# Where a discarded output and a normalised tile are kept, in a fused attention and gating kernel

## The chip, the cores and the metric

The kernel runs on one core of a Trainium2 chip. The metric is the device time of one execution in microseconds, read as the median of several executions. The engines have these names in the profile: PE (TensorE, matrix products; PEld is its loading of weights), DVE (VectorE), ACT (ScalarE), POOL (GpSimd) and SP (SyncE, which here only issues DMAs; ACT issues a few as well).

## The reference

Attention with 4 batches of 8 heads, 768 positions and 64 dimensions, in which a query sees only the keys of its own hash bucket, feeds a layer with spatial gating:

```python
q_bucket = sum((q @ proj > 0) * powers);  k_bucket = sum((k @ proj > 0) * powers)
scores = where(q_bucket == k_bucket, q @ k.T / 8, -1e9)
attn = exp(scores - max(scores));  attn = attn / (sum(attn) + 1e-9)
x = (attn @ v), heads side by side                     # 4 x 768 x 512
h = maximum(x @ w_in, 0);  u, v = halves of h          # 512 features each
v_n = (v - mean(v)) / sqrt(var(v) + 1e-6)              # over the features
v_s = w_spatial @ v_n + b_spatial                      # over the positions
out = (u * v_s) @ w_out
```

All inputs and the output are float32.

## The kernel before

**Number format.** Products run in float16, and a float32 operand is carried as two float16 parts, the rounded value and the remainder. Most steps therefore come as a cast on ACT that makes the first part and a subtraction on DVE or POOL that makes the second, called the split here.

**Attention.** There are 32 heads of 6 query tiles each (128 queries by 768 keys). A tile is named by head and row, 13_2 being row 2 of head 13. Heads 1 to 7 (`KEYS`) compute the scores with the keys on the partitions (`scores_k`) and need no transpose. Head 0 and heads 8 to 31, 150 tiles, go through `scores` and `weighted`:

1. L291 and L292: four products on PE put the scores into a PSUM tile `sp` (two of them).
2. L293: DVE scales `sp` by a negative constant and takes the minimum of each row into `nb`. The instruction also has to write its elementwise output somewhere: that is `jk`, a bfloat16 tile that nobody reads. There is one of it.
3. L295: ACT takes the exponential of `sp` with the bias `nb` into `ex`, float32, three buffers (`EB`).
4. L298 and L299: the cast on ACT and the split, on DVE or POOL, write the two halves of `pp`, three buffers (`PB`). POOL has rows 0 and 3 of heads below 16, and row 2 from head 16 on.
5. L301: SP issues a DMA that transposes `pp` into `pt`, five buffers (`PTB`). Heads 1 to 7 keep their exponentials under the same tag.
6. L314 to L316: 18 products on PE multiply `pt` with the values. They stand five tiles (`LAG`) behind the scores in the program.

**Gating layer.** When the 8 heads of a batch are done, `mlp_units` gives 28 units, which are dealt out among the tiles of the next batch. The last batch's units come after all attention. Six units (L361 to L370) make the half v: products, a rectifier on ACT (L365) into `v32m` (four buffers, which the output tiles of L436 use as well), then the statistics on DVE. After three of them `norm` normalises: DVE writes the result into `vy`, two buffers (L388), ACT casts it to the first part of `vn` (L389) and POOL subtracts to the second (L390). The other units make u (L402), the spatial product (L417) and the output (L432).

**Order.** The program is written tile by tile, and each step has a priority that the function `at` sets. A scheduler then fixes the order of the instructions on each engine when the program is built. A tile of a pool that has `bufs` buffers waits for the last reader of the tile `bufs` allocations earlier. On the chip each engine works through its own list in order and waits by semaphores.

Of the kernel before, what the change touches and what calls it, by code (L numbers as in the profile page):

```python
# [10 lines left out]
BF16 = mybir.dt.bfloat16  # L11
F32 = mybir.dt.float32
# [3 lines left out]
ALU = mybir.AluOpType  # L16
# [3 lines left out]
P = 128  # L20
# [16 lines left out]
def lsh_attention_spatial_gating(  # L37
# [11 lines left out]
    nc = tc.nc  # L49
    B, NPAIR, _, _, S = kq.shape  # L50
    NH = 2 * NPAIR
    NT = S // P
    HS = S // 2
    DM = NPAIR * P
    DF = w_in.shape[1]
    F2 = DF // 2
    NF = F2 // P
    ISQ = 1.0 / (SQ * SQ * 8.0)

    VYB = 2  # L60
    QKB = 1
    PSB = (2,2,2)
    MT = "m"
# [2 lines left out]
    wk = ctx.enter_context(tc.tile_pool(name="wk", bufs=1))  # L66
# [189 lines left out]
    def scores_k(n, i):  # L256
# [3 lines left out]
        for c in range(2):  # L260
            cs = slice(c * HS, (c + 1) * HS)
            nc.tensor.matmul(ps[:, c], lhsT=t[:, 1, ks], rhs=t[:, 0, cs], start=True, stop=False)  # L262
            nc.tensor.matmul(ps[:, c], lhsT=t[:, 2, ks], rhs=t[:, 3, cs], start=False, stop=True)  # L263
        ex = wk.tile([P, S], F32, tag="pt", bufs=PTB, name=f"ex{n}_{i}")
        st["ex", n, i] = nc.scalar.activation(ex.rearrange("p (c q) -> p c q", c=2), ps, AF.Exp, scale=ISQ).ins
# [12 lines left out]
    def scores(n, i):  # L278
        if n in KEYS:
            scores_k(n, i)  # L280
            return
        t = ab[n % NAB]
        if i == 0:
            st["nb", n] = wk.tile([P, NT], F32, tag="nb", bufs=3, name=f"nb{n}")
        nb = st["nb", n][:, i:i + 1]
        jk = wk.tile([P, 2, HS], BF16, tag="jk", name=f"jk{n}_{i}")
        qs = slice(i * P, (i + 1) * P)
        ps = ps_sc.tile([P, 2, 512], F32, tag="sc", name=f"sp{n}_{i}")[:, :, :HS]
        for c in range(2):
            cs = slice(c * HS, (c + 1) * HS)  # L290
            nc.tensor.matmul(ps[:, c], lhsT=t[:, 0, qs], rhs=t[:, 1, cs], start=True, stop=False)  # L291
            nc.tensor.matmul(ps[:, c], lhsT=t[0:P - 1, 3, qs], rhs=t[0:P - 1, 2, cs], start=False, stop=True)  # L292
        nc.vector.tensor_scalar(jk, ps, -ISQ, None, op0=ALU.mult, op1=ALU.min, accum_out=nb)  # L293
        ex = wk.tile([P, 2, HS], F32, tag="ex", bufs=EB, name=f"ex{n}_{i}")
        st["ex", n, i] = nc.scalar.activation(ex, ps, AF.Exp, bias=nb, scale=ISQ).ins  # L295
        at(NT * n + i + G_H, 50)
        pp = wk.tile([P, 2, 2, HS], F16, tag="pp", bufs=PB, name=f"pp{n}_{i}")
        nc.scalar.copy(pp[:, 0], ex)  # L298
        (nc.gpsimd if i in (PL_POOL if n >= 2 * NH else PL_POOL1) else nc.vector).tensor_tensor(out=pp[:, 1], in0=ex, in1=pp[:, 0], op=ALU.subtract)  # L299
        pt = st["pt", n, i] = wk.tile([P, 2 * NT, P], F16, tag="pt", bufs=PTB, name=f"pt{n}_{i}")  # L300
        st["tr"] = nc.sync.dma_start_transpose(out=pt, in_=pp.rearrange("p g c k -> p (g c k)")).ins  # L301
# [48 lines left out]
    def mlp_units(b):  # L350
        xt = [st["xt", b * NPAIR + r] for r in range(NPAIR)]
        vn = [wk.tile([P, NT, F2], F16, tag=f"vn{g}", name=f"vn{b}_{g}") for g in range(2)]
        mv = {}
        v32 = {}

        def v_unit(i):
            ps = ps_m.tile([P, 512], F32, tag=MT, name=f"vps{b}_{i}")
            k = 0
            for c in range(NPAIR):
                for gx, gw in THREE:  # L360
                    nc.tensor.matmul(ps, lhsT=xt[c][:, gx, i * P:(i + 1) * P], rhs=wi[gw][:, c, F2:DF],  # L361
                                     start=(k == 0), stop=(k == 3 * NPAIR - 1))
                    k += 1
            v32[i] = wk.tile([P, F2], F32, tag="v32m", bufs=4, name=f"vr{b}_{i}")
            nc.scalar.activation(v32[i], ps, AF.Relu, scale=1.0 / (SX * SX))  # L365
            if i % 3 == 0:
                mv[i // 3] = wk.tile([P, 3, 2], F32, tag="mv", bufs=2, name=f"mv{b}_{i}")
            bs = wk.tile([P, 6], F32, tag="bs", bufs=2, name=f"bs{b}_{i}")
            nc.vector.bn_stats(bs, v32[i])
            nc.vector.bn_aggr(mv[i // 3][:, i % 3, :], bs)  # L370
            if i % 3 == 2:
                norm(i // 3)

        def norm(g):
            m = mv[g]
            ve = wk.tile([P, 3], F32, tag="ve", bufs=2, name=f"ve{b}_{g}")
            nc.vector.tensor_scalar(ve, m[:, :, 1], EPS_LN, None, op0=ALU.add)
            r = wk.tile([P, 3], F32, tag="rs", bufs=2, name=f"rs{b}_{g}")
            nc.scalar.activation(r, ve, AF.Ln)
            nc.scalar.activation(r, r, AF.Exp, scale=-0.5)  # L380

            nc.vector.tensor_mul(ve, ve, r)
            nc.vector.scalar_tensor_tensor(out=ve, in0=ve, scalar=-0.5 * SN, in1=r, op0=ALU.mult, op1=ALU.mult)
            nc.vector.scalar_tensor_tensor(out=r, in0=ve, scalar=1.5 * SN, in1=r, op0=ALU.add, op1=ALU.mult)
            for j in range(3):
                i = 3 * g + j
                y = wk.tile([P, F2], F32, tag="vy", bufs=VYB, name=f"vy{b}_{i}")
                nc.vector.tensor_scalar(y, v32[i], m[:, j, 0:1], r[:, j:j + 1], op0=ALU.subtract, op1=ALU.mult)  # L388
                nc.scalar.copy(vn[0][:, i], y)  # L389
                nc.gpsimd.tensor_tensor(out=vn[1][:, i], in0=y, in1=vn[0][:, i], op=ALU.subtract)  # L390

        u = {}

        def u_unit(d, h):
            if h not in u:
                u[h] = wk.tile([P, NF, HS], F32, tag="u", name=f"u{b}_{h}")
            hs = slice(h * HS, (h + 1) * HS)
            ps = ps_m.tile([P, 512], F32, tag=MT, name=f"ups{b}_{d}_{h}")
            k = 0
            for c in range(NPAIR):  # L400
                for gw, gx in THREE:
                    nc.tensor.matmul(ps[:, :HS], lhsT=wi[gw][:, c, d * P:(d + 1) * P], rhs=xt[c][:, gx, hs],  # L402
                                     start=(k == 0), stop=(k == 3 * NPAIR - 1))
                    k += 1
            nc.scalar.activation(u[h][:, d], ps[:, :HS], AF.Relu, scale=1.0 / SX)  # L405

        gt = {}

        def s_unit(d, h):
            if h not in gt:  # L410
                gt[h] = [wk.tile([P, NF, HS], F16, tag=f"g{g}", name=f"g{b}_{g}_{h}") for g in range(2)]
            hs = slice(h * HS, (h + 1) * HS)
            ps = ps_m.tile([P, 512], F32, tag=MT, name=f"sps{b}_{d}_{h}")
            k = 0
            for c in range(NT):
                for gv, gw in THREE:
                    nc.tensor.matmul(ps[:, :HS], lhsT=vn[gv][:, c, d * P:(d + 1) * P], rhs=ws[gw][:, c, hs],  # L417
                                     start=(k == 0), stop=(k == 3 * NT - 1))
                    k += 1
            y = wk.tile([P, HS], F32, tag="sy", bufs=2, name=f"sy{b}_{d}_{h}")  # L420
            nc.vector.scalar_tensor_tensor(out=y, in0=ps[:, :HS], scalar=1.0 / (SN * SW), in1=bt[:, hs], op0=ALU.mult, op1=ALU.add)  # L421
            nc.gpsimd.tensor_mul(y, y, u[h][:, d])  # L422
            nc.scalar.copy(gt[h][0][:, d], y)
            nc.gpsimd.tensor_tensor(out=gt[h][1][:, d], in0=y, in1=gt[h][0][:, d], op=ALU.subtract)

        def o_unit(i):
            h, j = divmod(i, NT // 2)
            ps = ps_m.tile([P, 512], F32, tag=MT, name=f"ops{b}_{i}")
            k = 0
            for c in range(NF):  # L430
                for gg, gw in THREE:
                    nc.tensor.matmul(ps, lhsT=gt[h][gg][:, c, j * P:(j + 1) * P], rhs=wo[gw][:, c, :],  # L432
                                     start=(k == 0), stop=(k == 3 * NF - 1))
                    k += 1
            o = wk.tile([P, DM], F32, tag="v32m", bufs=4, name=f"o{b}_{i}")
            nc.scalar.activation(o, ps, AF.Copy, scale=1.0 / (SX * SX))  # L436
            nc.sync.dma_start(out=out[b, i * P:(i + 1) * P, :], in_=o)

        units = [lambda i=i: v_unit(i) for i in range(NT)]
        for h in range(2):  # L440
            units += [lambda d=d, h=h: u_unit(d, h) for d in range(NF)]
            units += [lambda d=d, h=h: s_unit(d, h) for d in range(NF)]
            units += [lambda i=i: o_unit(i) for i in range(h * NT // 2, (h + 1) * NT // 2)]
        return units
# [17 lines left out]
        return 99  # L462

    RB = 3
    PB = 3
    EB = 3
    PTB = 5
    XTB = 6
    LAG = 5
    XL_ENG = nc.vector  # L470
# [33 lines left out]
    for g in range(N * NT + LAG):  # L504
        n, i = divmod(g, NT)
        if n < N:
            at(g + G_S, 0)
            scores(n, i)
            r = n // 2
# [38 lines left out]
        while wv < N * NT and wv + (LAGK if wv // NT in KEYS else LAG) <= g:  # L548
            m, j = divmod(wv, NT)
# [64 lines left out]
```

## Time and profile before

| | |
|---|---|
| three executions | 738.57 us median (736.13 to 741.49) |
| span of the profiled execution | 741.7 us |
| PE busy | 631.5 us (85%) |
| DVE busy | 520.6 us (70%) |
| ACT busy | 434.8 us (59%) |
| POOL busy | 321.2 us (43%) |
| DMA moved | 120.95 MB, 163 GB/s in the mean |
| L293, minimum into `jk` | 150 on DVE, 949 ns each |
| L295, exponential | 150 on ACT, 897 ns each |
| L298, cast into `pp` | 150 on ACT, 829 ns each |
| L299, split into `pp` | 116 on DVE, 1089 ns each; 34 on POOL, 1708 ns each |
| L388, normalised v into `vy` | 24 on DVE, 860 ns each |
| L390, second part of `vn` | 24 on POOL, 1300 ns each |

Busy time is the time in which at least one instruction of the engine ran. The profiled execution is one of its own. Its span lies 3.1 us above the median of the three executions. Where a row of the profile says how long an engine idled, the name behind the arrow is the event that came last before the engine went on.

### The profile page before, as it was taken

The numbers are of one execution on the slowest core, as the hardware profiler recorded it, in microseconds if no ns is written. First come the engines' busy times: TensorE is split into PE (matmuls) and PEld (weight loads), VectorE is DVE, ScalarE is ACT, GpSimd is POOL, SyncE is SP. The second block draws the span as 40 slices with busy tenths as digits, with TensorE's granted clock in tenths as the row PEclk, the third lists the DMA queues.
The fourth block names the chain that finished last, engine by engine and source line by source line (L and its number), as shares of the span: only waits on it lengthen the run. The fifth ranks groups of instructions, "written<-read, shape, count | busy, mean of one in ns | idle before, by whom it ended". The sixth has DMA issues, their size and how long they took to land.

```text
span 741.7 us, 14927 instructions
## 1 busy us (share of the span) xinstructions
PE 631.5 (85%) x5759; PEld 400.4 (54%) x5759; DVE 520.6 (70%) x945; ACT 434.8 (59%) x668; POOL 321.2 (43%) x324
## 2 busy tenths in 40 slices
PE   1569898998988776997898899889898998999997
PEld 0237686776445444554544555556455565654553
DVE  4677795536799999567689798678698987755200
ACT  1344574346788676655676577667677776743221
POOL 5122443123458675264314565156235571451503
PEclk9768797999999989898999999999999999999999
DMA  9565554324999989996999799999999999860011
GB/s 235 149 123 155 133 148 102 99 55 97 224 237 197 215 207 187 213 178 138 234 202 199 138 210 213 211 211 212 206 210 181 194 175 213 182 136 15 1 42 43
DMA packets 290011, 120.95 MB, mean 163 GB/s; under 512 B 270740, under 2 KB 273812, under 8 KB 289940
## 3 DMA queue, kind: packets, MB, share of 16 engines
q1 hardware_dynamic: 287636, 119.11, 76.4%
q10 hardware_dynamic: 2304, 0.89, 0.5%
q8 instruction: 45, 0.74, 0.4%
q14 instruction: 26, 0.21, 0.1%
HBM read 28.33 MB, written 6.29 MB: 47 GB/s over the span
## 4 chain that ended last, share of the span: by engine, by line
PE 43%; DMA 21%; DVE 13%; issue 8%; ACT 6%; POOL 6%; SPq 3%; ACTq 0%; DVEq 0%; POOLq 0%
DMA pt<-pp 14%; PE pv L275 6%; PE vps L361 6%; PE ops L432 5%; PE sps L417 5%; PE ups L402 5%; DMA ab<-hl 4%; PE sp L291 3%; DVE jk L293 3%; PE sp L292 3%; DVE pp L299 2%; PE sp L262 2%; PE pv L314 2%; ACT ex L295 2%; PE sp L263 2%
## 5 line engine op out<-in xcount | busy, mean ns | idle before, releaser
L295 ACT ACTIVATE ex<-sp,nb 128x768 f32<-128x768 f32 x150 | 134.1, 897 | 54.8 <-DVE jk L293 48.9
L299 DVE TENSOR_TENSOR pp<-ex,pp 128x768 f16<-128x768 f32 x116 | 126.2, 1089 | 47.6 <-ACT pp L298 46.5
L293 DVE TENSOR_SCALAR_CACHE_REDUCE jk<-sp 128x768 bf16<-128x768 f32 x150 | 142.4, 949 | 24.1 <-PE sp L292 22.2
L298 ACT CAST pp<-ex 128x768 f16<-128x768 f32 x150 | 124.3, 829 | 50.0 <-DMA pt<-pp 43.9
L314 PE MATMUL pv<-vp,pt 128*128 128x65 f16 x900 | 108.2, 198 | 40.5 <-DMA pt<-pp 40.2
L291 PE MATMUL sp<-ab 128*128 128x384 f16 x300 | 103.2, 344 | 31.6 <-ACT ex L295 19.3
L314 PEld LDWEIGHTS <-pt 128*128 128x128 f16 x900 | 86.7, 101 | 67.2 <-DMA pt<-pp 53.4
L299 POOL TENSOR_TENSOR pp<-ex,pp 128x768 f16<-128x768 f32 x34 | 58.1, 1708 | 131.1 <-ACT pp L298 124.6
L315 PE MATMUL pv<-vp,pt 128*128 128x64 f16 x900 | 108.0, 197 | 0.0
L316 PE MATMUL pv<-vp,pt 128*128 128x65 f16 x900 | 107.8, 198 | 0.0
L292 PE MATMUL sp<-ab 127*128 127x384 f16 x300 | 103.9, 346 | 0.0
L417 PE MATMUL sps<-ws,vn 128*128 128x384 f16 x576 | 100.9, 329 | 1.5 <-DVE sg L180 1.0
L315 PEld LDWEIGHTS <-pt 128*128 128x128 f16 x900 | 87.0, 100 | 11.3 <-issue 1.3
L316 PEld LDWEIGHTS <-pt 128*128 128x128 f16 x900 | 86.9, 100 | 3.1 <-issue 0.5
L417 PEld LDWEIGHTS <-vn 128*128 128x128 f16 x576 | 55.3, 99 | 37.8 <-issue 3.9
L432 PE MATMUL ops<-wo,g 128*128 128x512 f16 x288 | 70.9, 391 | 1.5 <-ACT o L436 0.9
L275 PEld LDWEIGHTS pv<-vf,ex 128*128 128x128 f32 x504 | 68.5, 208 | 4.1 <-issue 1.6
L402 PE MATMUL ups<-xt,wi 128*128 128x384 f16 x384 | 69.1, 333 | 1.3 <-ACT u L405 0.9
L361 PE MATMUL vps<-wi,xt 128*128 128x512 f16 x288 | 68.0, 383 | 1.4 <-DMA xt<-xs 1.3
L275 PE MATMUL pv<-vf,ex 128*128 128x65 f32 x504 | 67.0, 286 | 0.0
L333 POOL TENSOR_TENSOR x<-x,xf 128x384 f32<-128x384 f32 x32 | 35.5, 1110 | 64.1 <-DVE x L332 64.1
L422 POOL TENSOR_TENSOR sy<-sy,u 128x384 f32<-128x384 f32 x32 | 36.6, 1145 | 49.3 <-DVE sy L421 49.2
(87 smaller groups left out, 1010.7 us busy)
## 6 DMA issues: line engine op xcount, KB each, us to landing
qk<-kq SPq DMA_DIRECT2D x16, 768.0 KB
ab<-hl SPq DMA_DIRECT2D x31, 384.0 KB
ab<-hl SPq DMA_DIRECT2D x34, 192.0 KB
out<-o SPq DMA_DIRECT2D x24, 256.0 KB
v<-v SPq DMA_DIRECT2D x13, 384.0 KB
raw<-w_in SPq DMA_DIRECT2D x16, 256.0 KB
pt<-pp SPq DMA_TRANSPOSE x150
raw<-w_sp SPq DMA_DIRECT2D x12, 192.0 KB
```

Of the source, the lines that this page charges most:

```text
L275: nc.tensor.matmul(acc[:, qi, :], lhsT=ex[:, qi * P:(qi + 1) * P], rhs=vf[p % 2][:, 2 * i + e, :], start=(i == 0 and qi == 0), stop=(i == ...
L291: nc.tensor.matmul(ps[:, c], lhsT=t[:, 0, qs], rhs=t[:, 1, cs], start=True, stop=False)
L292: nc.tensor.matmul(ps[:, c], lhsT=t[0:P - 1, 3, qs], rhs=t[0:P - 1, 2, cs], start=False, stop=True)
L293: nc.vector.tensor_scalar(jk, ps, -ISQ, None, op0=ALU.mult, op1=ALU.min, accum_out=nb)
L295: st["ex", n, i] = nc.scalar.activation(ex, ps, AF.Exp, bias=nb, scale=ISQ).ins
L298: nc.scalar.copy(pp[:, 0], ex)
L299: (nc.gpsimd if i in (PL_POOL if n >= 2 * NH else PL_POOL1) else nc.vector).tensor_tensor(out=pp[:, 1], in0=ex, in1=pp[:, 0], op=ALU.subtract)
L314: nc.tensor.matmul(acc, lhsT=pt[:, c, :], rhs=vh, start=(i == 0 and c == 0), stop=False)
L315: nc.tensor.matmul(acc[:, 0:D], lhsT=pt[:, c, :], rhs=vl, start=False, stop=False)
L316: nc.tensor.matmul(acc, lhsT=pt[:, NT + c, :], rhs=vh, start=False, stop=(i == NT - 1 and c == NT - 1))
L361: nc.tensor.matmul(ps, lhsT=xt[c][:, gx, i * P:(i + 1) * P], rhs=wi[gw][:, c, F2:DF], start=(k == 0), stop=(k == 3 * NPAIR - 1))
L417: nc.tensor.matmul(ps[:, :HS], lhsT=vn[gv][:, c, d * P:(d + 1) * P], rhs=ws[gw][:, c, hs], start=(k == 0), stop=(k == 3 * NT - 1))
```

## The change

The minimum's discarded output is written into the first half of the tile that the same tile's exponential will fill, so `jk` goes. The normalised v overwrites the rectified v in `v32m`, so `vy` goes. `pp` gets a fourth buffer and `pt` a sixth.

```diff
-    VYB = 2
...
-        jk = wk.tile([P, 2, HS], BF16, tag="jk", name=f"jk{n}_{i}")
+        ex = wk.tile([P, 2, HS], F32, tag="ex", bufs=EB, name=f"ex{n}_{i}")
+        jk = ex.rearrange("p c k -> p (c k)").bitcast(BF16)[:, 0:S].rearrange("p (c k) -> p c k", c=2)
...
         nc.vector.tensor_scalar(jk, ps, -ISQ, None, op0=ALU.mult, op1=ALU.min, accum_out=nb)
-        ex = wk.tile([P, 2, HS], F32, tag="ex", bufs=EB, name=f"ex{n}_{i}")
         st["ex", n, i] = nc.scalar.activation(ex, ps, AF.Exp, bias=nb, scale=ISQ).ins
...
-                y = wk.tile([P, F2], F32, tag="vy", bufs=VYB, name=f"vy{b}_{i}")
-                nc.vector.tensor_scalar(y, v32[i], m[:, j, 0:1], r[:, j:j + 1], op0=ALU.subtract, op1=ALU.mult)
+                y = v32[i]
+                nc.vector.tensor_scalar(y, y, m[:, j, 0:1], r[:, j:j + 1], op0=ALU.subtract, op1=ALU.mult)
...
-    PB = 3
+    PB = 4
     EB = 3
-    PTB = 5
+    PTB = 6
```

The number of instructions that compute stays the same on every engine; their order moves, most of all in heads 9 to 14. In the rows below, a name ends in a serial number that means nothing; `sp13_1` is the scores of tile 13_1, `w` and `raw` are weights in preparation, `xs` and `x` the attention's output.

DVE at the start of head 13, before: the minimums of 13_1 and 13_2 stand ahead of the splits of 12_4 and 12_5.

```order
L293 TENSOR_SCALAR jk13_1_3161,nb13_3122<-sp13_1_3162 128x768
L139 TENSOR_SCALAR w33_2789<-w33_2789 128x256
L299 TENSOR_TENSOR pp12_4_3024<-ex12_4_3022,pp12_4_3024 128x768
L140 TENSOR_SCALAR w33_2789<-w33_2789 128x256
L339 TENSOR_TENSOR xs5_2714<-x11_3055,xs5_2714 128x6x64
L141 SCALAR_TENSOR_TENSOR w33_2789<-raw33_2660,w33_2789 128x256
L139 TENSOR_SCALAR w34_2837<-w34_2837 128x256
L293 TENSOR_SCALAR jk13_2_3211,nb13_3122<-sp13_2_3212 128x768
L142 SCALAR_TENSOR_TENSOR w33_2789<-raw33_2660,w33_2789 128x256
L299 TENSOR_TENSOR pp12_5_3071<-ex12_5_3069,pp12_5_3071 128x768
```

The same place of the changed kernel (its lines are one lower from the second row of the diff on, and the minimum writes `ex`):

```order
L298 TENSOR_TENSOR pp12_4_2983<-ex12_4_2975,pp12_4_2983 128x768
L331 TENSOR_TENSOR x11_3014<-pv11_2732,rv11_3010 128x384
L141 SCALAR_TENSOR_TENSOR w33_2753<-raw33_2626,w33_2753 128x256
L218 SCALAR_TENSOR_TENSOR vp1_95<-v32_7_2458,vp1_95 128x12x64
L298 TENSOR_TENSOR pp12_5_3029<-ex12_5_3021,pp12_5_3029 128x768
L293 TENSOR_SCALAR ex13_1_3118,nb13_3080<-sp13_1_3119 128x768
L293 TENSOR_SCALAR ex13_2_3167,nb13_3080<-sp13_2_3168 128x768
```

Both splits now stand ahead of the minimums of the tiles three later.

ACT in head 18, before, where the first group of a batch's v is normalised:

```order
L295 ACTIVATE ex18_3_4748<-sp18_3_4742,nb18_4582 128x768
L298 CAST pp18_3_4750<-ex18_3_4748 128x768
L295 ACTIVATE ex18_4_4795<-sp18_4_4789,nb18_4582 128x768
L389 CAST vn1_0_4211<-vy1_0_4470 128x512
L365 ACTIVATE vr1_4_4634<-vps1_4_4621 128x512
L389 CAST vn1_0_4211<-vy1_1_4474 128x512
L365 ACTIVATE vr1_5_4716<-vps1_5_4703 128x512
L298 CAST pp18_4_4797<-ex18_4_4795 128x768
```

The same place of the changed kernel:

```order
L388 CAST vn1_0_4146<-vr1_0_4204 128x512
L388 CAST vn1_0_4146<-vr1_1_4294 128x512
L388 CAST vn1_0_4146<-vr1_2_4387 128x512
L294 ACTIVATE ex18_3_4660<-sp18_3_4661,nb18_4507 128x768
L364 ACTIVATE vr1_4_4558<-vps1_4_4545 128x512
L294 ACTIVATE ex18_4_4706<-sp18_4_4707,nb18_4507 128x768
L297 CAST pp18_3_4668<-ex18_3_4660 128x768
L364 ACTIVATE vr1_5_4638<-vps1_5_4625 128x512
L297 CAST pp18_4_4714<-ex18_4_4706 128x768
```

The three casts of the normalised v (`vr` itself now) come first, and the rectifiers `vr1_4` and `vr1_5` behind them; the casts of attention follow the exponentials as before.

POOL at the same point of head 18, before, where the second parts of the normalised v are made:

```order
L390 TENSOR_TENSOR vn1_1_4212<-vy1_0_4470,vn1_0_4211 128x512
L333 TENSOR_TENSOR x17_4828<-x17_4828,xf17_4821 128x384
L390 TENSOR_TENSOR vn1_1_4212<-vy1_1_4474,vn1_0_4211 128x512
L225 TENSOR_TENSOR va10_4851<-v32_10_4329 128x384
L324 TENSOR_SCALAR fl18_5103<-nb18_4582 128x6
L227 TENSOR_TENSOR vc10_4853<-va10_4851 128x128
L390 TENSOR_TENSOR vn1_1_4212<-vy1_2_4478,vn1_0_4211 128x512
```

The same place of the changed kernel:

```order
L389 TENSOR_TENSOR vn1_1_4147<-vr1_0_4204,vn1_0_4146 128x512
L389 TENSOR_TENSOR vn1_1_4147<-vr1_1_4294,vn1_0_4146 128x512
L389 TENSOR_TENSOR vn1_1_4147<-vr1_2_4387,vn1_0_4146 128x512
L332 TENSOR_TENSOR x17_4745<-x17_4745,xf17_4738 128x384
L323 TENSOR_SCALAR fl18_5014<-nb18_4507 128x6
L224 TENSOR_TENSOR va10_4767<-v32_10_4261 128x384
```

The three subtractions now stand in one run.

## The prediction

> **What bounds the kernel now.** I read the windows first, cut where the work changes: heads 0 to 7 until 173 us, heads 8 to 31 until 662 us, the last batch's dense layers after that. Columns are the stretch's length, the busy time of the five engines with their counts, the granted TensorE clock, the DMA share and GB/s.
>
> ```profile
> core 0: us, PE busy (x) PEld busy (x) DVE busy (x) ACT busy (x) POOL busy (x), PEclk, DMA share, GB/s
> 0.00:173.00 173.00, 133.27 (x936) 99.03 (x937) 107.09 (x201) 77.67 (x125) 54.18 (x79) 0.86 0.52 129
> 173.00:300.00 127.00, 99.80 (x986) 60.78 (x985) 117.28 (x203) 96.03 (x158) 79.97 (x72) 0.92 0.98 206
> 300.00:662.00 362.00, 323.42 (x3436) 201.12 (x3435) 280.08 (x507) 240.36 (x345) 164.18 (x152) 0.97 0.97 192
> 662.00:742.00 80.00, 75.02 (x406) 39.46 (x404) 16.12 (x35) 20.71 (x42) 22.88 (x23) 0.99 0.10 35
> ```
>
> The changed buffers serve the two middle stretches. From 173 to 300 us VectorE works 117.3 of 127 us: it bounds there, and a shorter wait elsewhere buys little. From 300 to 662 us no engine is full: TensorE works 323.4 of 362 us and idles 38.6, VectorE idles 82. So second, what TensorE, ScalarE and VectorE wait for after 300 us (total, times, longest), and the cast's wait before 300 us last:
>
> ```profile
> PE pv L314 <- DMA pt<-pp: 20.1, 18, 2.9
> PE sp L291 <- ACT ex L295: 9.1, 7, 5.1
> ...
> ACT pp L298 <- DMA pt<-pp: 39.6, 27, 3.7
> ...
> DVE pp L299 <- ACT pp L298: 45.0, 28, 4.2
> ...
> ACT pp L298 <- DMA pt<-pp: 4.3, 6, 2.0
> ```
>
> The cast (L298) writes the split buffer `pp`, of which there are three, so it stands until the transpose of the tile three before has landed: 39.6 us in 27 casts. ScalarE takes its work in order, so the next exponential stands behind it; VectorE's split (L299) then waits 45.0 us for the cast, the transpose goes out late, and TensorE pays at both ends, 20.1 + 9.1 = 29.2 us.
>
> Third, the chain that ended last, in order of time. It goes through landed transposes in two ways:
>
> ```profile
> 378.60 6.79 DMA pt<-pp
> ...
> 385.41 0.02 ACTq L298
> ...
> 395.85 8.67 DMA pt<-pp
> ...
> 404.57 0.20 PE pv L314
> ```
>
> At 378.60 the landing releases a cast: a buffer was missing. At 395.85 it releases the product itself: that wait is the transfer, and no `pp` buffer shortens it. After 300 us the chain takes the first way seven times and the second six; before 300 us, once each.
>
> **The change part by part.**
>
> *Fourth split.* The cast of tile m now waits for the landing of m-4. At the eight crossings of the first kind, the brackets tell how long ScalarE stood:
>
> ```profile
> 244.34 0.83 ACT L298 CAST pp<-ex 128x768 f16<-128x768 f32 x1 [1.24 <-DMA pt<-pp]
> 320.05 0.83 ACT L298 CAST pp<-ex 128x768 f16<-128x768 f32 x1 [3.00 <-DMA pt<-pp]
> 385.47 0.83 ACT L298 CAST pp<-ex 128x768 f16<-128x768 f32 x1 [1.50 <-DMA pt<-pp]
> 431.80 0.83 ACT L298 CAST pp<-ex 128x768 f16<-128x768 f32 x1 [1.19 <-DMA pt<-pp]
> 524.12 0.83 ACT L298 CAST pp<-ex 128x768 f16<-128x768 f32 x1 [3.65 <-DMA pt<-pp]
> 564.80 0.83 ACT L298 CAST pp<-ex 128x768 f16<-128x768 f32 x1 [2.79 <-DMA pt<-pp]
> 588.41 0.83 ACT L298 CAST pp<-ex 128x768 f16<-128x768 f32 x1 [0.44 <-DMA pt<-pp]
> 615.47 0.83 ACT L298 CAST pp<-ex 128x768 f16<-128x768 f32 x1 [1.25 <-DMA pt<-pp]
> ```
>
> The seven after 300 us sum to 13.8 us, with the first one 15.1. The 108 tiles of heads 14 to 31 take 362/108 = 3.4 us each here and the longest stand is 3.7 us, so one tile's respite removes nearly all of them. Bounds: 0, if the next wait is just as late; 29.2 us, if every wait of TensorE after 300 us goes. I take -15.1. Next late are the products' own waits and VectorE's order.
>
> *Minimum's output into the exponential's tile.* No instruction is added. But `jk` was never read, while the tile of `ex` (three of them) is read by cast and split; so the minimum of m (L293) now waits for the split of m-3, which before only the exponential did. Behind it stand all of VectorE's work and, through `nb`, the exponential. From tile 9_1 to tile 14_2, 12 minimums began before that split was done; the first and the last, each with its split and exponential:
>
> ```profile
> 189.81 0.96 DVE L293 TENSOR_SCALAR_CACHE_REDUCE jk<-sp 128x768 bf16<-128x768 f32 x1 [0.29 <-PE sp L292]
> 190.69 0.95 DVE L299 TENSOR_TENSOR pp<-ex,pp 128x768 f16<-128x768 f32 x1
> ...
> 191.94 0.89 ACT L295 ACTIVATE ex<-sp,nb 128x768 f32<-128x768 f32 x1
> ...
> 300.93 0.95 DVE L293 TENSOR_SCALAR_CACHE_REDUCE jk<-sp 128x768 bf16<-128x768 f32 x1
> 301.81 0.08 DVE L293 DVE_READ_ACCUMULATOR jk<-sp 128x1 f32 x1
> ...
> 302.27 0.95 DVE L299 TENSOR_TENSOR pp<-ex,pp 128x768 f16<-128x768 f32 x1
> ...
> 303.50 0.91 ACT L295 ACTIVATE ex<-sp,nb 128x768 f32<-128x768 f32 x1
> ```
>
> In the last, the split ends at 303.22, the minimum would end at 303.22 + 0.95 + 0.08 = 304.25 and the exponential start 0.75 later than its 303.50. At most every one of the 12 pays a whole minimum, 12 x 1.03 = 12.4 us; at least 0, since VectorE only swaps two pieces of work and stays busy. The casts come earlier too. I take +2.5, near the lower end, as VectorE has work for 92% of this stretch (117.3 of 127).
>
> *Normalised v in place.* No instruction is added or removed. The two `vy` tiles go; the `v32m` tile (four) is now held until POOL's subtraction of `vn` (L390), so ScalarE's rectifier four units on (L365) waits for that, with casts and exponentials queued behind it. The dearest place:
>
> ```profile
> 403.49 1.15 POOL L390 TENSOR_TENSOR vn<-vy,vn 128x512 f16<-128x512 f32 x1 [5.20 <-ACT vn L389]
> ...
> 405.55 1.42 POOL L390 TENSOR_TENSOR vn<-vy,vn 128x512 f16<-128x512 f32 x1
> ...
> 403.31 0.60 ACT L365 ACTIVATE vr<-vps 128x512 f32<-128x512 f32 x1
> ...
> 404.31 0.61 ACT L365 ACTIVATE vr<-vps 128x512 f32<-128x512 f32 x1
> ```
>
> The two rectifiers would start at 404.64 and 406.97: 2.7 us of delay in all. In the new order POOL does these subtractions in one run, ahead of `x` and `va`, so less. It happens once a batch; the last batch is the tightest for TensorE, and there the first subtraction ends within 0.2 us of the rectifier it now holds:
>
> ```profile
> 678.59 2.27 POOL L390 TENSOR_TENSOR vn<-vy,vn 128x512 f16<-128x512 f32 x2 [15.72 <-ACT vn L389]
> ...
> 679.61 0.60 ACT L365 ACTIVATE vr<-vps 128x512 f32<-128x512 f32 x1 [0.57 <-PE vps L361]
> ```
>
> Bounds 0 and 4 x 2.7 = 10.8 us; I take +1, near 0, since ScalarE idles a third of the time (362 - 240.4 = 121.6 us after 300 us) and absorbs it.
>
> *Sixth transposed buffer.* The queue's own list speaks for a gain, the times against one:
>
> ```profile
> SPq L301 <- PE pv L316: 57.0, 41, 3.2
> ...
> 640.69 4.56 SPq L301 DMA_TRANSPOSE pt<-pp  x3
> ...
> 637.37 0.19 PE L314 MATMUL pv<-vp,pt 128*128 128x65 f16 x1
> ```
>
> The second of these three transposes, tile 31_0's, reuses the buffer of 30_1, whose products ran around 637.4 to 638.0, four microseconds before. Over all 144 tiles the buffer was free at least 4.2 us ahead; the releaser named is only the last event, and the queue was waiting for the split or busy issuing. I take 0. Heads 1 to 7 share the tag, but their exponentials wait for scores, not for a buffer: 0 too.
>
> **Sum:** -15.1 + 2.5 + 1 + 0 = -11.6 us. The profiled execution spans 741.7 us, at the slow end of the three times (736.13 to 741.49); for one like it 730.1, for the median of 738.57, **727.0**.
>
> **The rivals.**
>
> *DMA is the bound.* Its share is 0.97, so transposes sent sooner would only lie longer. For it: landings took 6.79 and 8.67 us above, while the first of the program, nearly alone, took 3.54.
>
> ```profile
> 28.65 3.54 DMA pt<-pp
> ```
>
> Against it: the GB/s of the same rows move between 192 and 206, and the queue waits for splits with nothing to issue. Then cast waits shrink, product waits grow by as much: 738.6 less a quarter of 11.6, some 736. [...]
>
> *All waits of TensorE go, and its clock rises.* 29.2 us of waits after 300 us, and the granted clock of 0.97 becomes the 0.99 of the last stretch: 323.42 x (1 - 0.97/0.99) = 6.5 us. 738.6 - 35.7 = 703. For it: one late tile delays the next through the same buffers. Against it: six of thirteen crossings are the transfer itself. [...]
>
> *Minimum queued behind the split: slower.* From 173 to 300 us VectorE is the bound, and there a minimum that stands for a split that itself waits for a cast idles the full engine. It decides if VectorE's busy time there falls below today's 117 of 127 us. With all 12 paying and the buffer gaining nothing: 738.6 + 12.4 = 751; halved by the earlier casts, 745.
>
> *The change does not do what it says.* Order on each engine is set at build; were the casts placed no earlier, the fourth buffer would idle. ScalarE's order keeps exponential and cast of a tile together, as before, and the only wait ahead of a cast that can bind is the buffer's, so I give this no time of its own.
>
> **How the numbers follow.** Forecast 0.50 (718 to 733), DMA rival 0.22, full relief 0.10, slower 0.18. About 1% is what a measurement of this kernel tells from no change: below 731.2 lie most of the forecast (0.46) and the full relief, 0.56; within 1% the rest of the forecast, most of the DMA rival and the mild half of the slower one, 0.30; above 746 the rest, 0.14. The range goes from the relief of all waits without clock (738.6 - 29.2 = 709) to 748, just short of the full price of the slower rival.
>
> **What would show it.** Right: the cast's wait for DMA after 300 us falls below 10 us, VectorE's wait for casts below 25, TensorE's two waits from 29 to about 15; the middle stretch ends some 11 us sooner and the last keeps its 75 us of TensorE. Wrong: product waits that grow by what the casts lose (DMA), a new wait of the minimum for splits or POOL (slower), or rectifiers that wait for POOL for more than 3 us in all.

## The result and the profile after

The changed kernel takes **729.96 us** in the median of four executions (724.46 to 730.27), beside 738.33 us (736.13 to 741.49) of the kernel before: a ratio of 0.988, with an interval of 0.983 to 0.9925. The forecast was 727.0. Ratios and intervals, here and below, are taken from the undisturbed executions of both kernels, medians from all. The profiled execution spans 727.9 us, 13.8 less than the one of before.

The windows of the changed kernel, with the columns of before:

```profile
0.00:173.00 173.00, 133.74 (x978) 98.93 (x979) 110.69 (x208) 80.72 (x129) 54.75 (x80) 0.92 0.54 133
173.00:300.00 127.00, 99.56 (x1035) 59.37 (x1034) 120.31 (x206) 98.53 (x165) 83.99 (x73) 0.93 1.03 214
300.00:662.00 362.00, 328.34 (x3414) 201.65 (x3411) 277.97 (x504) 238.07 (x342) 165.85 (x150) 0.98 0.96 191
662.00:728.00 66.00, 61.24 (x342) 33.20 (x340) 11.42 (x30) 16.90 (x35) 21.99 (x22) 1.00 0.07 25
```

From 300 to 662 us TensorE still idles 33.7 us (38.6 before). The granted clock rose in the first stretch from 0.86 to 0.92, where only the six tiles of head 0, and the first of head 8 at its end, use the split buffers.

The waits of the changed kernel after 300 us (total, times, longest); L294 is the exponential here, L293 the minimum, L297 the cast, L298 the split:

```profile
ACT ex L294 <- DVE ex L293: 58.4, 50, 3.6
DVE ex L293 <- PE sp L292: 32.0, 23, 3.6
...
PE pv L313 <- DMA pt<-pp: 22.1, 20, 3.4
DVE pp L298 <- ACT pp L297: 19.7, 19, 3.4
...
PE sp L291 <- ACT ex L294: 6.1, 6, 1.7
```

The cast's 39.6 us for DMA fell to 1.1 us in one cast, and the split's 45.0 us for casts fell to 19.7. But TensorE's two waits, 29.2 us before, are 22.1 + 6.1 = 28.2 us. The time that ScalarE and VectorE no longer spend on a buffer they spend further up: the exponential waits 58.4 us for minimums (26.6 before) and the minimum 32.0 us for scores (12.6 before).

At this point the forecast looks nearly confirmed: the total is close and the cast is free. The experiments show that it came out of terms that were not right one by one.

### The profile page after: what moved, and what is told of

It is laid out like the page before. It is cut to its first block, busy times and chain, and to the rows that moved or that the text cites. A ratio compares the mean times of both kernels' runs of the same rounds, so it can differ in the third digit from the quotient of the medians.

```text
span 727.9 us, 14930 instructions
## 1 busy us (share of the span) xinstructions
PE 622.9 (86%) x5759; PEld 393.2 (54%) x5759; DVE 520.4 (71%) x945; ACT 434.2 (60%) x668; POOL 326.6 (45%) x324
## 5 line engine op out<-in xcount | busy, mean ns | idle before, releaser
L294 ACT ACTIVATE ex<-sp,nb 128x768 f32<-128x768 f32 x150 | 134.6, 900 | 95.3 <-DVE ex L293 91.2
L293 DVE TENSOR_SCALAR_CACHE_REDUCE ex<-sp 128x768 bf16<-128x768 f32 x150 | 141.8, 949 | 43.2 <-PE sp L292 42.4
L298 DVE TENSOR_TENSOR pp<-ex,pp 128x768 f16<-128x768 f32 x116 | 125.9, 1091 | 20.7 <-ACT pp L297 20.5
L313 PE MATMUL pv<-vp,pt 128*128 128x65 f16 x900 | 105.5, 196 | 34.0 <-DMA pt<-pp 33.5
L297 ACT CAST pp<-ex 128x768 f16<-128x768 f32 x150 | 123.8, 830 | 10.6 <-ACT ex L294 2.5
L313 PEld LDWEIGHTS <-pt 128*128 128x128 f16 x900 | 85.4, 100 | 59.3 <-DMA pt<-pp 48.6
L298 POOL TENSOR_TENSOR pp<-ex,pp 128x768 f16<-128x768 f32 x34 | 58.2, 1711 | 123.9 <-ACT pp L297 101.1
L416 PE MATMUL sps<-ws,vn 128*128 128x384 f16 x576 | 103.9, 333 | 3.0 <-DVE sg L179 2.2
L314 PE MATMUL pv<-vp,pt 128*128 128x64 f16 x900 | 105.6, 195 | 0.0
L315 PE MATMUL pv<-vp,pt 128*128 128x65 f16 x900 | 105.3, 197 | 0.0
L292 PE MATMUL sp<-ab 127*128 127x384 f16 x300 | 102.4, 341 | 0.0
L314 PEld LDWEIGHTS <-pt 128*128 128x128 f16 x900 | 85.8, 99 | 10.7 <-issue 2.0
L315 PEld LDWEIGHTS <-pt 128*128 128x128 f16 x900 | 85.7, 99 | 3.7 <-issue 0.6
L274 PEld LDWEIGHTS pv<-vf,ex 128*128 128x128 f32 x504 | 65.6, 200 | 3.9 <-issue 1.1
L274 PE MATMUL pv<-vf,ex 128*128 128x65 f32 x504 | 64.5, 279 | 0.0
```

Of the source, the lines that this page charges most:

```text
L274: nc.tensor.matmul(acc[:, qi, :], lhsT=ex[:, qi * P:(qi + 1) * P], rhs=vf[p % 2][:, 2 * i + e, :], start=(i == 0 and qi == 0), stop=(i == ...
L313: nc.tensor.matmul(acc, lhsT=pt[:, c, :], rhs=vh, start=(i == 0 and c == 0), stop=False)
L314: nc.tensor.matmul(acc[:, 0:D], lhsT=pt[:, c, :], rhs=vl, start=False, stop=False)
L315: nc.tensor.matmul(acc, lhsT=pt[:, NT + c, :], rhs=vh, start=False, stop=(i == NT - 1 and c == NT - 1))
```

## The experiments

Each kernel was compared with runs of the kernel before on the same chip; the ratio is to those. All have five transposed buffers unless six are named.

**Both in-place edits, no new buffer** (`space_only`), on the changed kernel:

```diff
-    PB = 4
+    PB = 3
-    PTB = 6
+    PTB = 5
```

> Both in-place edits as in the change, but three split buffers and five transposed ones as before: the space is freed and not used. Theory (the gain is the fourth split buffer's, through the cast's waits): no gain, 738 to 745 us; after 300 us the cast still waits about 40 us for DMA and VectorE about 45 us for casts, and the minimum's new wait for splits costs 0 to 7 us. Rival (the new order of the instructions that the in-place edits bring, not the buffer): the time is that of the changed kernel, about 730 us, though the casts still wait 30 us or more.

Measured: 729.61 us (12 executions), ratio 0.9915 (0.9872 to 0.9958). Its waits after 300 us:

```profile
ACT pp L297 <- DMA pt<-pp: 41.0, 25, 4.1
DVE pp L298 <- ACT pp L297: 40.6, 32, 4.1
...
PE pv L313 <- DMA pt<-pp: 16.4, 20, 3.0
...
PE sp L291 <- ACT ex L294: 12.0, 16, 1.8
```

The cast waits as long as ever, 41.0 us, and yet the gain is there, as far as the intervals can tell: the rival holds. So the wait that the prediction was built on can stay without costing the gain.

**Fourth split, v in place, the minimum's own tile kept** (`split4_own_jk`), on the kernel before:

```diff
-                y = wk.tile([P, F2], F32, tag="vy", bufs=VYB, name=f"vy{b}_{i}")
-                nc.vector.tensor_scalar(y, v32[i], m[:, j, 0:1], r[:, j:j + 1], op0=ALU.subtract, op1=ALU.mult)
+                y = v32[i]
+                nc.vector.tensor_scalar(y, y, m[:, j, 0:1], r[:, j:j + 1], op0=ALU.subtract, op1=ALU.mult)
...
-    PB = 3
+    PB = 4
```

> The kernel before with v normalised in place and four split buffers; the minimum keeps its own discarded tile, and there are five transposed buffers. Theory: the whole gain of the fourth split without the minimum's new wait: 725 to 730 us, so equal to the changed kernel or up to 4 us faster; the cast's wait for DMA after 300 us falls below 10 us, and no minimum waits for a split. Rival (the minimum's wait costs nothing): within 1 us of the changed kernel, 729 to 731. Rival (order, not buffer): 735 us or more.

Measured: 732.60 us (12), ratio 0.9924 (0.9887 to 0.9960); the cast's wait after 300 us is 6.0 us. That lies between the two rivals. It is no faster than the changed kernel: that the minimum waits for splits there costs nothing that shows in two kernels whose orders differ as well.

**Five transposed buffers** (`pt5`), on the changed kernel:

```diff
-    PTB = 6
+    PTB = 5
```

> The changed kernel with five transposed buffers instead of six. Theory (the buffer was free 4 us ahead for every tile): the time of the changed kernel, 729 to 731 us, and no waits that grow by over 3 us in all. Rival (the sixth buffer carries part of the gain, since transposes go out earlier with four splits): 733 us or more, with the transposes' queue waiting for products.

Measured: 731.23 us (12), ratio 0.9925 (0.9886 to 0.9964), not to be told from the changed kernel. The queue names products as its last releaser for 58.5 us in 41 waits instead of 48.4 in 40, more than the 3 us that the theory allowed, and nothing comes of it. In the traces the two kernels have the same order of instructions on every engine.

**A fourth tile for the exponential** (`ex4_pt5`), on `pt5`:

```diff
-    EB = 3
+    EB = 4
```

> The changed kernel with five transposed buffers and, in their place, a fourth tile for the exponential, so that the minimum waits for the split of the tile four before instead of three. If the minimum's new wait costs time: 724 to 728 us, and the exponential's wait for minimums after 300 us falls from 58 us towards the 27 us of the kernel before. If it costs nothing (the minimum waits for scores, that is for TensorE): 729 to 731 us, and the exponential still waits some 50 us.

Measured: 727.34 us (6), ratio 0.9891 (0.9834 to 0.9948). The time fits the first case, the wait the second: the exponential still waits 52.1 us for minimums after 300 us (55.7 in `pt5`). The intervals overlap; this stays open.

**The minimum's edit alone, and the normalised v's alone** (`jk_in_ex_only`, `v_in_place_only`): on the kernel before, the first has only

```diff
-        jk = wk.tile([P, 2, HS], BF16, tag="jk", name=f"jk{n}_{i}")
+        ex = wk.tile([P, 2, HS], F32, tag="ex", bufs=EB, name=f"ex{n}_{i}")
+        jk = ex.rearrange("p c k -> p (c k)").bitcast(BF16)[:, 0:S].rearrange("p (c k) -> p c k", c=2)
```

and the second only the four lines on `y` shown above.

> Only the minimum's discarded output goes into the exponential's tile; everything else as before, three split buffers included. Both in-place edits together, without any new buffer, took 729.6 us. Theory 1 (this edit carries that gain, because the order that comes of it makes the minimum of a tile stand behind the splits and lets TensorE work more evenly, so that its clock is granted more often): 728 to 732 us, mean granted clock about 0.958 against 0.943 of the kernel before. Theory 2 (the other edit carries it): 735 to 740 us at 0.943.

> Only the normalised v is written in place; everything else as before. Theory 1 (the minimum's edit carries the gain of the two edits together): 736 to 740 us, granted clock about 0.943. Theory 2 (this edit carries it: casts and subtractions of the normalised v stand in one run, and rectifiers come earlier): 728 to 732 us, clock about 0.958. If both this kernel and the one with the minimum's edit alone lie between 731 and 736, the gain belongs to neither but to the order that each build happens to get.

Measured: 732.55 us (6), ratio 0.9891 (0.9849 to 0.9932), granted clock 0.953 in the mean; and 743.87 us (12), ratio 1.0026 (0.9986 to 1.0067), clock 0.947. The minimum's edit alone brings a gain, a little less than theory 1 said; the normalised v's brings none, and its median lies above either theory.

**The changed kernel without the normalised v in place** (`split4_vy`):

```diff
+    VYB = 2
...
-                y = v32[i]
-                nc.vector.tensor_scalar(y, y, m[:, j, 0:1], r[:, j:j + 1], op0=ALU.subtract, op1=ALU.mult)
+                y = wk.tile([P, F2], F32, tag="vy", bufs=VYB, name=f"vy{b}_{i}")
+                nc.vector.tensor_scalar(y, v32[i], m[:, j, 0:1], r[:, j:j + 1], op0=ALU.subtract, op1=ALU.mult)
...
-    PTB = 6
+    PTB = 5
```

> The changed kernel with the normalised v in its own two tiles again and five transposed buffers: the minimum in the exponential's tile and four split buffers are all that is left of the change. In place, the normalised v cost about 4 us on the kernel before (742.3 us in the mean of twelve runs against 738.7). Theory 1 (the three edits add up): some 4 us less than the changed kernel, 724 to 727 us. Theory 2 (four split buffers and the minimum's new place cure the same lateness, and it is only there that the normalised v in place hurts): as the changed kernel, 728 to 732 us. The mean granted clock tells whether a difference is the clock's: about 4.2 us for each 0.01.

Measured: **718.78 us** (6; 716.85 to 721.23), ratio **0.9758 (0.9713 to 0.9803)**. It beats both kernels, by more than theory 1 gave. After 300 us it and `jk_in_ex_only`, which differs from it in the fourth split alone, show what that buffer does here, first three splits, then four:

```profile
ACT pp L298 <- DMA pt<-pp: 40.9, 28, 4.1
...
PE pv L314 <- DMA pt<-pp: 15.2, 19, 2.0
PE sp L292 <- ACT ex L295: 13.3, 14, 2.2
```

```profile
PE pv L314 <- DMA pt<-pp: 15.7, 19, 2.3
...
PE sp L292 <- ACT ex L295: 4.8, 8, 1.8
...
ACT pp L298 <- DMA pt<-pp: 2.7, 4, 1.1
```

The cast is free, and TensorE's two waits fall from 28.5 to 20.5 us. Over the whole profile, span less busy time, TensorE idles 104.9 us with three splits and 92.5 with four: in this pair the buffer works in the way that the prediction described. Between `space_only` (105.6) and the changed kernel (105.0) it does not. The medians of the whole set, in us:

| | three splits | four splits |
|---|---|---|
| own tile for the minimum, own `vy` | 738.3 (before) | not tried |
| own tile for the minimum, v in place | 743.9 | 732.6 |
| minimum in `ex`, own `vy` | 732.6 | **718.8** |
| minimum in `ex`, v in place | 729.6 | 731.2 (with six `pt`: 730.0) |

Read along rows and columns, the effects don't add. The fourth split brings 13.8 us, 11.3 us or nothing (+1.6); v in place costs 5.5, gives back 2.9, or costs 12.4. Of these the 1.6, the 2.9 and the 5.5 are not clear of the noise by the ratios' intervals. In the traces every edit of this table moves the order of the instructions on all engines; only the sixth transposed buffer leaves it as it is. That an edit's effect is that of its order is the likeliest reading; no run here changes the order alone.

Heads 24 to 31 are one place where v in place may cost; first the changed kernel from the first scores of head 24 to the last products, its window and four waits, then the same of `split4_vy`:

```profile
489.00:649.00 160.00, 146.19 (x1580) 90.36 (x1577) 126.06 (x230) 109.26 (x159) 77.82 (x70) 0.99 0.96 187
...
POOL pp L298 <- ACT pp L297: 31.1, 7, 8.8
...
DVE ex L293 <- PE sp L292: 14.1, 10, 3.1
...
PE pv L313 <- DMA pt<-pp: 9.7, 12, 1.8
PE sp L291 <- ACT ex L294: 3.0, 2, 1.7
```

```profile
487.00:639.00 152.00, 142.69 (x1585) 89.33 (x1582) 128.99 (x234) 108.15 (x156) 79.10 (x70) 1.00 1.01 196
...
POOL pp L299 <- ACT pp L298: 15.0, 6, 7.6
...
PE pv L314 <- DMA pt<-pp: 5.8, 8, 1.9
...
DVE ex L294 <- PE sp L293: 4.4, 8, 1.3
...
PE sp L292 <- ACT ex L295: 1.2, 4, 0.5
```

The same heads take 8 us more in the changed kernel. POOL's splits wait twice as long for their casts, the products wait longer for transposes, and TensorE idles 13.8 us instead of 9.3. But `pt5`, which differs from `split4_vy` in v in place alone and has the changed kernel's order, takes 155.5 us for them, idles 11.8, and its POOL splits wait 33.8 us for casts. So half of the 8 us is not v in place, or comes and goes between executions. That the cause of the rest is the run of three `vn` casts ahead of exponentials and casts, which the order of ScalarE in head 18 shows, fits these rows but was not tried apart.

**Products six tiles behind the scores** (`lag6`), on the changed kernel:

```diff
-    LAG = 5
+    LAG = 6
```

> The changed kernel with the products of weights and values six tiles behind the scores instead of five. Theory (the products still wait about 22 us for landed transposes because five tiles are too few to cover the landing): that wait falls below 10 us after 300 us and the time by 3 to 8 us, to 722 to 727. Rival (the wait moves: with six transposed buffers a transpose then waits for products, or the scores wait for exponentials): the wait is found again in another row, and the time is 729 to 733 us.

In it the last tile of every second head is weighted with values of the pair two later, whose split stands ahead of it in the program; only its time is read. Measured: 722.29 us (6), ratio 0.9811 (0.9763 to 0.9860). After 300 us:

```profile
PE sp L291 <- ACT ex L294: 16.1, 13, 5.1
...
PE pv L313 <- DMA pt<-pp: 8.4, 10, 1.9
```

The product's wait falls from 22.1 to 8.4 us, as the theory has it, and 10.0 us of that come back as the scores' wait (6.1 to 16.1). The changed dependences of that one tile may have a share in the time, so the gain is not claimed.

**The granted clock.** The ratio of `space_only` had to come from somewhere, since the waits did not move. Its mean granted clock over twelve executions is 0.958; that of the kernel before, over the 57 executions that stood beside these runs, is 0.942. The traces record the clock in pieces of 3.41 us, each at full or at half speed (the third column from the right below, 1.00 or 0.50). The kernel before at two places, cut at the pieces' edges:

```profile
77.98:81.39 3.41, 1.92 (x16) 1.63 (x15) 1.64 (x3) 1.96 (x3) 1.70 (x3) 1.00 1.03 269
81.39:84.80 3.41, 2.83 (x12) 2.31 (x12) 3.41 (x5) 2.48 (x6) 3.41 (x5) 0.50 0.08 30
84.80:88.22 3.42, 3.42 (x17) 3.02 (x17) 2.45 (x8) 1.05 (x3) 2.16 (x3) 0.50 0.74 177
88.22:91.63 3.41, 3.41 (x13) 2.22 (x14) 0.87 (x3) 0.79 (x2) 0.00 (x0) 0.50 0.31 91
91.63:95.04 3.41, 3.15 (x25) 2.53 (x24) 2.96 (x5) 2.96 (x7) 0.98 (x2) 1.00 0.34 75
```

```profile
484.16:487.57 3.41, 0.54 (x17) 0.54 (x18) 1.93 (x4) 1.16 (x3) 3.25 (x5) 1.00 1.16 241
487.57:490.98 3.41, 3.41 (x33) 2.45 (x29) 2.91 (x5) 3.41 (x6) 0.35 (x1) 0.50 0.89 195
```

At the first, a piece with 1.92 us of TensorE's work is followed by three pieces at half speed, at the second a piece with 0.54 us by one. Over all pieces recorded in the fourteen traces of this case, a full-speed piece with under 1.2 us of TensorE's busy time was followed by a half-speed one in 79 of 79 cases, from 1.2 to 1.5 us in 58 of 61, from 1.5 to 1.7 in 32 of 45, from 1.7 to 2.0 in 7 of 82, above that in 1 of 2293. The edges of the pieces lay elsewhere in each trace, counted from the start of its span: one is at 118.89 us in the kernel before, one at 113.05 in the changed kernel and one at 116.22 in `warm_before`, which are 1.7 and 0.8 pieces earlier. So the same stand of TensorE can fall into one piece or be shared by two.

Three kernels fill one such stand, ahead of the product with the mean of v around 113 to 120 us (`warm_before`, `warm_after`, and `ex4_warm` with the fourth exponential tile):

```diff
+        for _ in range(8 if p == 3 else 0):
+            nc.tensor.matmul(mp[:, P:2 * P], lhsT=ones, rhs=a[:, 0:2].rearrange("p e d -> p (e d)"), start=True, stop=True)
         nc.tensor.matmul(mp[:, :P], lhsT=ones, rhs=c.rearrange("p e d -> p (e d)"), start=True, stop=True)
```

> The kernel before with the same eight idle products at the same place (around 120 us there). Theory: no half-clock piece there, and the same 3 to 5 us less as on the changed kernel: 733 to 735 us. If the change's whole gain came of this stretch and the one ahead of it, the difference between the two warmed kernels would fall below 4 us; if it comes of the buffers, it stays at 7 to 8 us. Rival (the half clock costs nothing there): 738 us.

> The changed kernel with eight idle products of 128x128 float32 (0.25 us each at full clock) on TensorE ahead of the product with the mean of v for heads 6 and 7, where TensorE stands for 2.3 us around 113 us; their results are written beside the product's and never read. Every profile so far shows the clock at half for two or three pieces of 3.41 us just behind this stand. Theory (a piece of 3.41 us in which TensorE works less than about 1.5 us brings half the clock in the next one): no half-clock piece between 112 and 130 us, and 3 to 5 us less than the changed kernel, 725 to 727 us. Rival (the half clock there costs nothing, or does not follow from the stand): the same half-clock pieces or no less time, 730 us or, by the added work, up to 732.

> The changed kernel with five transposed buffers, four exponential tiles and the eight idle products of 128x128 ahead of the product with the mean of v for heads 6 and 7. The four exponential tiles alone took 727.3 us in the median. Theory (the half-clock pieces behind the stand cost their full time, and what the exponential's tile brings does not depend on them): 723 to 726 us, no half-clock piece or one between 112 and 130 us. Rival (the next stand takes the time back): 727 to 730 us.

Measured: 731.88 us (6), ratio 0.9889 (0.9844 to 0.9934); 728.47 us (6), ratio 0.9852 (0.9816 to 0.9887); 731.34 us (6), ratio 0.9896 (0.9833 to 0.9959). The place in the kernel before, and in `warm_before`:

```profile
118.89:122.30 3.41, 0.49 (x2) 0.32 (x3) 0.70 (x1) 2.22 (x3) 2.37 (x5) 1.00 0.97 208
122.30:125.71 3.41, 3.39 (x15) 2.89 (x15) 2.71 (x5) 2.09 (x5) 0.91 (x1) 0.50 0.02 5
125.71:129.13 3.42, 3.42 (x18) 3.25 (x18) 1.72 (x3) 0.42 (x1) 0.00 (x0) 0.50 0.00 0
```

```profile
116.22:119.63 3.41, 2.66 (x22) 2.21 (x22) 2.18 (x2) 3.38 (x7) 1.62 (x5) 1.00 0.70 136
119.63:123.05 3.42, 1.99 (x16) 1.54 (x16) 3.35 (x7) 0.90 (x2) 1.00 (x1) 1.00 0.00 0
123.05:126.46 3.41, 3.41 (x29) 2.93 (x29) 1.54 (x2) 2.09 (x4) 0.67 (x1) 1.00 0.74 151
```

Of the half-speed pieces there are 0, 1 and 0 left there in the three kernels, against 2 or 3 in all the others: work whose results nobody reads kept the clock up. The one in `warm_after` follows a piece with 2.01 us of work. What the filled stand is worth in time is not settled: 7.5 us on the kernel before, more than expected; 1.5 us on the changed kernel, too little to be told; and `ex4_warm` is 4 us slower than `ex4_pt5`, above both its theories, though its mean clock is higher, 0.958 against 0.948. The two warmed kernels stand 3.4 us apart instead of 8.4, but their intervals overlap too far to say that the rest of the gain was this stretch's. One filled stand is not a gain to count on.

**A second profile of the kernel before** (`before_again`, no edit):

> The kernel before, unchanged, for a second profile. Theory (half-clock pieces fall by where the pieces of 3.41 us happen to begin, which differs between executions): the stretch of head 0 has other half-clock pieces than the first profile, the places around 80 and 120 us have two or three each again, and the starts of heads 8 to 31 differ from the first profile's by as much as the clock lost ahead of them, up to 6 us. Rival (the first profile is typical, and the changed kernel's gain of 5.7 us ahead of head 8 is its own): head 8 starts within 1.5 us of 173.0.

Measured: 740.02 us; two half-speed pieces at each of the two places; head 8 starts 3.6 us earlier than in the first profile. The window from 25 to 60 us in the first profile of before, in the second and in the changed kernel:

```profile
25.00:60.00 35.00, 22.68 (x150) 12.88 (x149) 22.08 (x30) 13.68 (x17) 7.59 (x8) 0.62 0.70 160
```

```profile
25.00:60.00 35.00, 23.76 (x163) 14.29 (x162) 22.99 (x34) 13.59 (x18) 8.08 (x10) 0.75 0.67 155
```

```profile
25.00:60.00 35.00, 24.51 (x175) 13.92 (x175) 23.33 (x35) 14.12 (x19) 8.06 (x10) 0.76 0.72 159
```

Of the 5.7 us by which head 8 begins earlier in the changed kernel's profile, 3.6 are the first profile's bad luck: one profile is good to several microseconds here, not better.

With a constant for each kernel and one common slope, all 151 timed executions give 4.0 us for 0.01 of mean granted clock (standard error 0.4). At equal clock the kernels then stand to the one before, in us with 95%: `space_only` -1.1 (2.1), `jk_in_ex_only` -1.1 (2.5), `v_in_place_only` +6.0 (1.8), `split4_own_jk` -3.3 (1.8), `pt5` -4.8 (1.8), the changed kernel -5.0 (2.9), `split4_vy` -14.7 (2.5). So the gain of the minimum's edit goes almost wholly with a higher granted clock, that of the fourth split mostly does not, and the changed kernel has about half of each. The profiles give a second account without the fit, TensorE's idle time over the whole span: 110.2 and 107.4 us in the two profiles of before, 104.9 in `jk_in_ex_only`, 105.6 in `space_only`, 105.0 in the changed kernel, 92.5 in `split4_vy`. It agrees that of these only `split4_vy` removes much of TensorE's waiting; it does not agree on `v_in_place_only` (109.7), which the fit puts 6 us behind. That the slope found within kernels holds between them is assumed: `ex4_warm` speaks against it. Since by the counts above a kernel with fewer stands also gets more clock, this parts the gain and does not name its first cause.

## Why the prediction was right and where it was not

**The total**, 727.0 with 709 to 748, holds the 730.0, and faster was the likeliest. That the total is off by only 3 us is luck: by the table below, a minimum 8.3 us better and a v in place 11.4 us worse than forecast nearly cancel. The terms were priced, in the main, by the waits that they add or take in the order of before; the new order, which every edit but the last brings, had no term. Each edit put on top of the ones ahead of it, they came out like this:

| term | predicted | measured | from |
|---|---|---|---|
| minimum into `ex` | +2.5 (0 to 12.4) | -5.8 | before to `jk_in_ex_only` |
| fourth split | -15.1 (-29.2 to 0) | -13.8 | to `split4_vy` |
| v in place | +1 (0 to 10.8) | +12.4 | to `pt5` |
| sixth transposed buffer | 0 | -1.3 | to the changed kernel, within its noise |

- **Fourth split: the size was right in one order only.** Beside the minimum's edit it brings 13.8 us, and by the way that was described: the cast's wait goes and TensorE idles less. With v in place too it brings nothing. (Added up by way of v in place, fourth split, minimum and sixth buffer, the same medians read +5.5, -11.3, -1.4 and -1.3.) What the prediction took from the chain, eight stands of the cast, all but went in the changed kernel; `space_only` shows that they need not go for 8 us to be gained.
- **Minimum: wrong sign.** The step that failed is the lower end of 0, "since VectorE only swaps two pieces of work". The wait itself stayed small: in the changed kernel's trace one of the 144 minimums from head 8 on, 11_4, begins as the split of three tiles before ends, 0.13 us behind it, since the new order has that split well ahead. In `jk_in_ex_only`, where the measured figure comes from, the minimum waits 2.3 us for POOL's splits, in two tiles, and the kernel is still faster. What else changed is the order, and the edit with it brought 5.8 us; of the 5.5 us between the means, 4.4 go with the clock by the fit above.
- **Normalised v: the wait that was priced hardly came, and the cost came without it.** The step priced two rectifiers that stand for POOL. The view of the tile `vr` of the changed kernel, with the idle time of its engines by what ended it:

```profile
  ACT vn L388: 18.4, 2
  PE vps L360: 11.4, 7
  ACT vr L364: 10.2, 5
  DVE vr L387: 5.3, 8
  PE pv L315: 0.8, 1
  POOL vn L389: 0.3, 1
```

  The rectifiers waited 0.3 us for POOL in the whole run, below the 3 us set as a sign. Yet the edit costs 12.4 us on `split4_vy`, above the upper bound of 10.8, which knew that one wait only. What costs the 12.4 us stays open; the run of `vn` casts named above is a candidate.
- **Sixth buffer: right**, for the reason given.
- **What was to show it:** the cast's wait below 10 us, right (1.1 us); the split's wait for casts below 25, right (19.7); TensorE's two waits from 29 to about 15, **wrong** (28.2); the middle stretch 11 us sooner, 11.3, but 5.7 of these lie ahead of head 8; the last stretch's TensorE work kept, nearly (73.4 us from the last product of attention on, 76.4 before).
- **Rivals.** DMA as the bound: product waits were to grow by what the casts lose, and they grew by 2.0 us where the casts lost 38.5; and `split4_vy` moves 203 GB/s from 300 to 645 us, where the kernel before and the changed one move 196, and is faster. The minimum behind the split as a slowdown: `split4_own_jk` without that wait is no faster. The change not doing what it says: the cast's wait went, so it did. Clock: the rival that had it rise did so only once all waits went; here it rises by 0.012 in the mean while TensorE's waits stay. The lower end of the range, 738.6 - 29.2 = 709, left the clock out, and no run shows that waits of 2.9 us cost none: the one at 484 us is followed by half speed, and so is a piece with 1.92 us of work.

## What to carry to other kernels

Where a scheduler fixes the order, price an edit by building and timing it apart, each alone and each left out: here three edits meant to belong together gave 1.2%, and leaving out the most harmless of them gave 2.4%. A wait that disappears from the list is not yet time: follow it to the engine that bounds, and if that engine's waits stay, the gain has another source. For a kernel bound by TensorE, set the mean granted clock of many executions beside every time, and take no difference of a few microseconds between two single profiles for the kernel's own.

## What the runs showed of the hardware

In the fourteen traces the clock that TensorE was granted changed at the edges of pieces of 3.41 us, and it went with how much TensorE worked in the piece before: with under 1.5 us of work, half speed followed in 137 of 140 cases, from 1.5 to 1.7 us in 32 of 45, above that in 8 of 2375. No gap as long as a piece was needed: ahead of 153 of the 177 drops, no stand of TensorE that touches the piece reached 3.41 us. Nor had the idle time to be in one stand: at 566.06 us of the kernel before, 1.8 us of it in a piece, in two stands of 1.44 and 0.39 us for transposes, were followed by half speed:

```profile
562.65:566.06 3.41, 1.59 (x27) 0.98 (x25) 0.90 (x2) 1.26 (x2) 3.25 (x6) 1.00 1.28 180
566.06:569.47 3.41, 3.09 (x40) 2.33 (x37) 3.41 (x8) 3.41 (x7) 1.71 (x2) 0.50 0.75 169
```

Once lowered, the clock stayed so for one to three pieces behind a stand in heads 1 to 31, and for up to five in the serial start (26.75 to 43.82 us in the kernel before). The executions of one and the same kernel, 729.85 to 745.74 us for the one before, went with it in part (a correlation of -0.64 over 57 executions): within kernels, 0.01 of mean clock was 4.0 us by the fit above.
